# The batch of several experts third, with only its other experts' tokens sorted

## The chip, the cores and the metric

One core of a Trainium2 chip runs the whole kernel. The metric is the time of one execution on the device in microseconds, taken over several runs. The profile is of one further execution; its span goes from the first to the last instruction.

## The reference

Four batches of 10048 tokens of width 128. First attention through 49 agents, then a mixture of 16 experts in four groups of four; each token goes to one group and in it to one expert.

```
a2k = softmax(scale * agents @ k.T);  agent_v = a2k @ v
x = softmax(scale * q @ agents.T) @ agent_v
g = argmax(x @ w_group);  e = argmax(x @ w_expert[g])
out = softmax_g * softmax_e * (relu(x @ w1[g, e]) @ w2[g, e])
```

The drawn inputs (seed 0) send all tokens of three batches to one expert each. The batch numbered 0 in the inputs has 7553 tokens for one expert, 2494 for a second and 1 for a third.

## The kernel before, in words

`PB` gives the order in which the input's batches are computed; below, "batch 0" to "batch 3" (`b`) are places in that order. A batch has 79 columns of 128 tokens, which make 20 FFN tiles of up to 512 tokens (`TILES`, L38).

**Attention.** `agents_of` (L401, lane kind "a") loads keys and values in ten chunks, splits them into two f16 parts on ScalarE (xh) and GpSimd (xl, L290), makes scores, and from them the agents' values. `rest` (L1101, lane kind "q") does the same for the queries (`queries_of`, L629; et is the transposed softmax of a tile), then routing logits, `routing` (L718), the choice of the batch's main expert (`main_of`, L827), the output weights (`output_weight`, L752), `peaks` (L945) and `signed_weights` (L971), which makes the FFN weights: 384 hidden units are computed exactly, the other 640 are taken as of one sign and folded into a linear part.

**FFN.** A tile has three units of `first` (L1119: ph on TensorE, relu to hh on ScalarE, the low part hl on VectorE) and `second` (L1135: po on TensorE), and five `check`s (L1156: pv on TensorE, then neg on ScalarE or a reduction into `flags` on VectorE) that the folded units kept their sign. `natural` (L1187) is a tile of tokens in their own order with the batch's main weights (wbuf); `rows_out` (L1196) scales it, on ScalarE and GpSimd (L1203) where `apart` is true and else on VectorE, and SP stores it (L1208).

**Batch 3 before.** The batch of several experts is last. `taken` (L1481) sorts all its tokens by expert: `leftover` (L1217) gives each token a place by scans, `inverse` (L1340) turns places into row numbers with one-hot products for 82 columns of 128, and up to three experts' weights are made by `prepare_kept` (L1415) and stored in DRAM (wkept). `fetch` (L1420) gathers a tile's rows with four indirect DMAs (er, L1426), `turn` (L1452) transposes them, `scatter` (L1462) stores with four more (L1467). Each is followed by a small memset of gap (`apart`, L1446), and the queue's order is kept. There are 20 whole tiles and one small one; up to five are gathered ahead, and each loads its weights anew from DRAM (`weigh`, L1448).

**What sets the order.** The FFN tiles of batch b are written out one after another, and work of the other lanes is laid between their steps by `run` (L1600) and `advance` (L1573). A lane has a span in units of batches (`SPAN_A`, `SPAN_Q`, `SPAN_O`, `SPAN_F`, L103), a total (`WORK`, L109), and a count of what it has issued: `Counted` (L144) prices each instruction (VectorE 65 + 1.04 per element of a partition, ScalarE 100 + 0.83, TensorE 4 + 0.42), and `WA` weighs TensorE, VectorE and ScalarE. At each step a lane is taken on until its count reaches its share of the total; when its span is over, all that is left of it is issued at once:

```
part = min(1.0, (now - y["start"]) / (y["end"] - y["start"]))
advance(y, part if part < 1 else 1e9, False)
```

Lane "f" is what is left of batch 0's queries and routing, lane "o" is `taken`. The front (to about 86 us) computes batch 0's attention by a written list (`ORDER`). Batches 0 and 1 have 20 natural tiles each, batch 2 has 13 in the same way; then the remaining lanes are finished, and the 21 taken tiles follow with the last seven natural ones of batch 2 among them. While the first two of these tiles run, `prepare_kept` makes the second and third experts' weights. At the end `general` (L1501) looks whether any flag is set or any count was over its limit (`KEPT`, `WHOLE`), and redoes the batches concerned if so.

Of the kernel before, what the change touches and what calls it, by code (L numbers as in the profile page):

```python
# [22 lines left out]
P = 128  # L23
B = 4
# [35 lines left out]
PB = [1, 2, 3, 0]  # L60
LB = B - 1
WHOLE = 20
TAKEN = WHOLE + 1
SOON = TAKEN * TQ
AWAY = 100
KEPT = 3
# [15 lines left out]
BESIDE = 7  # L82
# [20 lines left out]
SPAN_A = {1: (0.3, 0.7), 2: (0.97, 1.4), 3: (1.66, 1.98)}  # L103
SPAN_Q = {1: (0.53, 0.96), 2: (1.34, 1.78), 3: (1.93, 2.34)}
SPAN_O = (2.34, 2.62)
SPAN_F = (0.0, 0.52)
MIX = 2
WA = (0.3, 1.0, 0.3)
WORK = {"a": 25e3, "q": 42e3, "o": 35.7e3, "f": 38e3}  # L109
# [66 lines left out]
def build(ctx, tc, qT, kT, v, agT, wr, w1, w2, cpk, out):  # L176
    nc = tc.nc
    pool, sync = nc.gpsimd, nc.sync
    work = np.zeros(3)
# [43 lines left out]
    flags = const.tile([P, B, TAKEN, SLOTS], F32, name="flags")  # L223
# [30 lines left out]
    pool.memset(wbuf[1], 0)  # L254
# [71 lines left out]
    def key_scores(b, ci):  # L326

        st = state[b]
        S, mch = st["S"], st["mch"]
        t0, t1 = chunks[ci]  # L330
        xh, xl = st.pop(("k", ci))
        ps = bank(b)
        full = t1 - t0 - (1 if t1 == NT else 0)
        for t in range(t0, t1):
            scores(b, ps, xh, xl, t - t0, min(P, N - t * P))
            if t % 4 == 3:
                yield
        act.activation(S[:, t0:t0 + full], ps[:, 0:full * NA].rearrange("p (t a) -> p t a", a=NA), AF.Copy)
        psv = ps[:, 0:(t1 - t0) * NA].rearrange("p (t a) -> p t a", a=NA)
        vec.tensor_reduce(out=mch[:, ci % 2], in_=psv[:, 0:full].rearrange("p t a -> p a t"), axis=AX.X, op=ALU.max)  # L340
        if t1 == NT:
            act.activation(S[0:LAST, NT - 1], psv[0:LAST, full], AF.Copy)
            vec.tensor_max(out=mch[0:LAST, ci % 2], in0=mch[0:LAST, ci % 2], in1=psv[0:LAST, full])
# [324 lines left out]
    def query_split(b, ci, x, early):  # L668
        t0, t1 = chunks[ci]
        ef = x["ef"][:, 0:t1 - t0]  # L670
        if early and ci % 2 == 0:
            pool.tensor_copy(out=rows[:, t0:t1, 0:NA], in_=ef)
        else:
            act.activation(rows[:, t0:t1, 0:NA], ef, AF.Copy)
        whole = early or b == 0 and ci <= FIRST
        for i in range(0, t1 - t0, t1 - t0 if whole else 3):
            y = slice(i, t1 - t0 if whole else min(i + 3, t1 - t0))
            w = slice(t0 + y.start, t0 + y.stop)
            (vec if whole else pool).tensor_sub(out=rows[:, w, NA:2 * NA], in0=ef[:, y], in1=rows[:, w, 0:NA])  # L679
        yield  # L680

    def query_turn(b, ci, x, early):
        t0, t1 = chunks[ci]
        for h0 in range(t0, t1, TQ):
# [4 lines left out]
            et = (mo.tile([2 * NA, TS], F16, name="ett", bufs=4) if b == LB else etp.tile([2 * NA, TS], F16, name="et"))[:, 0:(h1 - h0) * P]  # L689
# [205 lines left out]
    def left_of(b, ps):  # L895
# [4 lines left out]
        lf = sm.tile([1, 2], F32, name="lf")  # L900
        vec.tensor_reduce(out=lf[:, 0:1], in_=lm, axis=AX.X, op=ALU.add)
        vec.tensor_scalar(out=lf[:, 0:1], in0=lf[:, 0:1], scalar1=-1.0, scalar2=float(N), op0=ALU.mult, op1=ALU.add)
        if b:
            vec.tensor_max(out=lf[:, 1:2], in0=lf[:, 0:1], in1=state[b - 1]["info"][:, 1:2])
        else:
            vec.tensor_copy(out=lf[:, 1:2], in_=lf[:, 0:1])
        info = const.tile([1, 2], I32, name=f"info{b}")
# [193 lines left out]
    def rest(b):  # L1101

        if b == LB:
            yield from queries_of(b, None, None, logits_of)
        else:
# [90 lines left out]
    def rows_out(x):  # L1196
# [14 lines left out]
        for y in ins:  # L1211
            if b < LB:
                tc.declare_no_dep(y.ins, group="taken", reason="those rows are of the last batch")
# [206 lines left out]
    def fetch(b, j, name="slot"):  # L1420
# [41 lines left out]
    def scatter(x):  # L1462
# [3 lines left out]
        for q in range(n):  # L1466
# [6 lines left out]
            if group == "taken":  # L1473
                tc.declare_no_dep(ins.ins, group="natural", reason="the rows are of the last batch, or none")
# [26 lines left out]
    def general():  # L1501
# [36 lines left out]
        pe.matmul(ps[:, 0:B * TAKEN], ones16, wrong, start=True, stop=True)
        state["right"] = const.tile([P, B, TAKEN], F16, name="right")
        psb = ps[:, 0:B * TAKEN].rearrange("p (b w) -> p b w", w=TAKEN)  # L1540
        vec.tensor_scalar(out=state["right"], in0=psb, scalar1=0.0, scalar2=None, op0=ALU.is_equal)
# [44 lines left out]
    def lane(kind, b, gen, span):  # L1586
        lanes.append(dict(kind=kind, b=b, gen=gen, start=span[0], end=span[1], total=WORK[kind] - (6.5e3 if kind == "q" and b == LB else 0), done=0.0, until=0.0))
# [10 lines left out]
    lane("o", LB, taken(LB), SPAN_O)  # L1598
    lanes.sort(key=lambda y: y["start"])
    def run(x, at=None, then=None, also=None):  # L1600

        steps = plan(x)
        for k, (kind, i) in enumerate(steps):
# [15 lines left out]
            for y in lanes:  # L1619
                if now > y["start"]:  # L1620
# [7 lines left out]
        if also:  # L1628
            all_of(also)
# [54 lines left out]
```

## Time and profile before

| what | us |
|---|---|
| median of three runs | 991.37 |
| lowest and highest of them | 990.78, 993.18 |
| the profiled execution | 987.76 |
| its span | 985.9 |
| TensorE busy in the span | 745.1 |
| VectorE busy | 700.1 |
| ScalarE busy | 481.3 |
| GpSimd busy | 499.0 |

PE is TensorE, PEld its weight loads, DVE VectorE, ACT ScalarE, POOL GpSimd, SP the engine that issues most DMAs. A window of the profile gives the busy time of each engine in it and the mean clock granted to TensorE as a share of its full speed. Nearly all compute instructions are recorded under one line (L160, the helper that counts them), so groups are told apart by the names of their tiles.

### The profile page before, as it was taken

The numbers are of one execution on the slowest core, as the hardware profiler recorded it, in microseconds if no ns is written. First come the engines' busy times: TensorE is split into PE (matmuls) and PEld (weight loads), VectorE is DVE, ScalarE is ACT, GpSimd is POOL, SyncE is SP. The second block draws the span as 40 slices with busy tenths as digits, with TensorE's granted clock in tenths as the row PEclk, the third lists the DMA queues.
The fourth block names the chain that finished last, engine by engine and source line by source line (L and its number), as shares of the span: only waits on it lengthen the run. The fifth ranks groups of instructions, "written<-read, shape, count | busy, mean of one in ns | idle before, by whom it ended". The sixth has DMA issues, their size and how long they took to land.

```text
span 985.9 us, 22607 instructions
## 1 busy us (share of the span) xinstructions
PE 745.1 (76%) x8802; PEld 556.5 (56%) x8802; DVE 700.1 (71%) x1738; ACT 481.3 (49%) x892; POOL 499.0 (51%) x805
## 2 busy tenths in 40 slices
PE   7839988999638998957669797479385887676873
PEld 5738656676436766744457575247374664454552
DVE  7787979767985867497755559997966774544553
ACT  5445766785413858936314894234122543333431
POOL 3342357470221919638501672113580588888885
PEclk9959999998858999987779899679787998878887
DMA  9562336731640754146505311332111442332321
GB/s 346 202 239 82 98 125 200 219 99 37 235 154 22 200 182 126 34 153 232 175 26 160 86 47 47 141 103 68 30 37 44 147 124 83 93 101 74 109 73 50
DMA packets 61893, 118.32 MB, mean 120 GB/s; under 512 B 7062, under 2 KB 38888, under 8 KB 61392
## 3 DMA queue, kind: packets, MB, share of 16 engines
q1 hardware_dynamic: 56592, 109.55, 34.2%
q0 software_dynamic: 5184, 7.23, 2.9%
q8 instruction: 71, 1.16, 0.5%
q14 instruction: 46, 0.38, 0.1%
HBM read 84.90 MB, written 32.01 MB: 119 GB/s over the span
## 4 chain that ended last, share of the span: by engine, by line
POOL 21%; PE 19%; DVE 14%; issue 4%; DMA 3%; ACT 3%; POOLq 0%; SPq 0%; DVEq 0%; ACTq 0%
PE at L160 10%; POOL out L1467 6%; POOL er L1426 5%; POOL xl L290 5%; PE po L160 4%; PE ph L160 3%; POOL gap L1446 3%; PE pv L160 2%; DVE hl L160 2%; DVE spare L160 1%; POOL rows L679 1%; POOL oo L1203 1%; DMA er<-erow,gidx 1%; DMA xf<-qT 1%; DVE pm L160 1%
## 5 line engine op out<-in xcount | busy, mean ns | idle before, releaser
L290 POOL TENSOR_TENSOR xl<-xf,xh 128x256 f16<-128x256 f32 x280 | 187.5, 702 | 168.6 <-ACT xh L160 167.7
L160 DVE SCALAR_TENSOR_TENSOR hl<-ph,hh 128x512 f16<-128x512 f32 (+1 forms) x241 | 163.4, 679 | 127.0 <-ACT hh L160 125.6
L160 ACT ACTIVATE hh<-ph 128x512 f16<-128x512 f32 (+1 forms) x241 | 142.8, 594 | 118.3 <-PE ph L160 117.5
L160 PEld LDWEIGHTS <-hh 128*128 128x128 f16 x1908 | 162.1, 103 | 38.2 <-issue 6.6
L160 PE MATMUL po<-wbuf,hh 128*128 128x128 f16 x1572 | 170.3, 228 | 0.4 <-ACT hh L160 0.3
L160 PE MATMUL po<-wbuf,hl 128*128 128x128 f16 x786 | 152.9, 228 | 18.3 <-DVE hl L160 18.3
L160 DVE CUSTOM_DVE_ANT_0 spare<-neg,pv 128x512 bf16<-128x512 bf16 (+1 forms) x160 | 107.8, 674 | 33.2 <-PE pv L160 27.7
L1203 POOL TENSOR_TENSOR oo<-oo,cw 128x256 f32<-128x256 f32 (+1 forms) x62 | 43.5, 722 | 166.2 <-ACT oo L160 166.2
L160 PE MATMUL ph<-et,wbuf 98*128 98x512 f16 (+1 forms) x360 | 117.6, 407 | 5.8 <-DVE hl L160 3.3
L160 PE MATMUL pv<-et,wbuf 98*128 98x512 f16 (+1 forms) x300 | 112.2, 407 | 10.3 <-DVE flags L160 3.7
L160 ACT ACTIVATE neg<-pv 128x512 bf16<-128x512 f32 (+1 forms) x160 | 95.0, 594 | 50.4 <-PE pv L160 49.2
L160 PEld LDWEIGHTS <-hl 128*128 128x128 f16 x954 | 98.3, 103 | 34.3 <-DVE hl L160 25.5
L1467 POOL DMA_INDIRECT out<-oo,sidx x81 | 80.7, 997 | 48.6 <-DVE oo L160 35.2
L160 PEld LDWEIGHTS <-wbuf 98*128 98x128 f16 x737 | 67.1, 104 | 54.7 <-issue 32.4
L160 ACT ACTIVATE xh<-xf 128x1024 f16<-128x1024 f32 x78 | 81.7, 1049 | 26.8 <-PE at L160 8.9
L1426 POOL DMA_INDIRECT er<-erow,gidx x81 | 83.3, 1029 | 20.4 <-issue 14.3
L160 PEld LDWEIGHTS <-xh 128*128 128x128 f16 x1264 | 62.7, 99 | 19.1 <-issue 8.7
L160 PE MATMUL at<-agh,xl 128*128 128x49 f16 x545 | 58.5, 189 | 13.1 <-POOL xl L290 12.5
L160 PEld LDWEIGHTS <-xl 128*128 128x128 f16 x632 | 53.1, 98 | 22.7 <-POOL xl L290 20.1
L160 PE MATMUL at<-agh,xh 128*128 128x49 f16 x545 | 59.0, 189 | 6.2 <-ACT xh L160 3.1
L160 DVE TENSOR_REDUCE flags<-pv 128x1 f32<-128x512 f32 (+1 forms) x82 | 55.1, 674 | 7.8 <-PE pv L160 7.6
L160 PEld LDWEIGHTS <-et 98*128 98x128 f16 x948 | 47.7, 99 | 20.3 <-issue 10.5
(384 smaller groups left out, 1567.2 us busy)
## 6 DMA issues: line engine op xcount, KB each, us to landing
xf<-qT SPq DMA_DIRECT2D x38, 512.0 KB, 5.2
vf<-v SPq DMA_DIRECT2D x36, 516.0 KB, 4.1
xf<-kT SPq DMA_DIRECT2D x35, 512.0 KB, 4.4
out<-oo SPq DMA_DIRECT2D x57, 256.0 KB, 2.3
erow<-rows SPq DMA_DIRECT2D x3, 1975.0 KB
wsl<-wkept SPq DMA_DIRECT2D x7, 608.0 KB, 3.6
wsg<-wkept SPq DMA_DIRECT2D x7, 608.0 KB
wbuf<-wkept SPq DMA_DIRECT2D x7, 608.0 KB, 3.6
```

The costliest lines, as they stand in the source:

```text
L160: y = f(*a, **k)
L290: eng.tensor_sub(out=xl[:, y], in0=xf[:, y], in1=xh[:, y])
L679: (vec if whole else pool).tensor_sub(out=rows[:, w, NA:2 * NA], in0=ef[:, y], in1=rows[:, w, 0:NA])
L1203: pool.tensor_mul(out=o[:, y], in0=o[:, y], in1=state[b]["cw"][:, t + y.start:t + y.stop].broadcast_to([P, y.stop - y.start, C]))
L1426: ins = pool.indirect_dma_start(out=er[:, q], out_offset=None, in_=erow[b][:, :], in_offset=bass.IndirectOffsetOnAxis(ap=place(b, col + q) ...
L1446: tc.keep_in_program_order(pool.memset(gap, 0.0))
L1467: ins = pool.indirect_dma_start(out=out, out_offset=bass.IndirectOffsetOnAxis(ap=place(x["b"], x["col"] + q)[1], axis=0), in_=o[:, q], in_ ...
```

## The change

The batch of several experts comes third (`MB`). Like the others it runs 20 natural tiles with the weights of its main expert, for all its tokens. `taken(MB)` then sorts the tokens of its other experts alone: five whole tiles and a small one, two kept weights. Their results are scattered over the rows that the natural tiles wrote. This lane "o" lies beside batch 3's tiles 0 to 11, and one taken tile follows each of batch 3's natural tiles 13 to 18. All four batches now take the same path through `rest`. The lanes' spans, totals and weights are new, and GpSimd's instructions for splitting are counted too (`half`). A lane's predecessor is finished as soon as the lane starts.

```diff
-PB = [1, 2, 3, 0]
+PB = [1, 2, 0, 3]
 LB = B - 1
-WHOLE = 20
+MB = B - 2
+WHOLE = 5
 TAKEN = WHOLE + 1
-SOON = TAKEN * TQ
+SOON = 84
-KEPT = 3
+KEPT = 2
-BESIDE = 7
+FROM = 13
...
-SPAN_A = {1: (0.3, 0.7), 2: (0.97, 1.4), 3: (1.66, 1.98)}
-SPAN_Q = {1: (0.53, 0.96), 2: (1.34, 1.78), 3: (1.93, 2.34)}
-SPAN_O = (2.34, 2.62)
-SPAN_F = (0.0, 0.52)
+SPAN_A = {1: (0.1, 0.42), 2: (0.96, 1.25), 3: (1.96, 2.25)}
+SPAN_Q = {1: (0.42, 0.96), 2: (1.25, 1.96), 3: (2.25, 2.96)}
+SPAN_O = (3.0, 3.55)
+SPAN_F = (0.0, 0.25)
-WA = (0.3, 1.0, 0.3)
-WORK = {"a": 25e3, "q": 42e3, "o": 35.7e3, "f": 38e3}
+WA = (0.3, 1.0, 0.5, 0.5)
+WORK = {"a": 41.3e3, "q": 98.6e3, "o": 80.5e3, "f": 37e3}
...
+    half = Counted(nc.gpsimd, work, 3, 80.0, 2.3)
-    flags = const.tile([P, B, TAKEN, SLOTS], F32, name="flags")
+    flags = const.tile([P, B, NW + TAKEN, SLOTS], F32, name="flags")
-        low(pool, PIECE, xf, xh, xl, n)
+        low(half, PIECE, xf, xh, xl, n)
...
-            st["mch"] = sm.tile([P, 2, NA], F32, name="mch")
+            st["mch"] = rt.tile([P, len(chunks), NA], F32, name="mch", tag="hot")
...
-        if ci:
-            vec.tensor_max(out=mch[:, ci % 2], in0=mch[:, ci % 2], in1=mch[:, 1 - ci % 2])
...
-        mx = st["mch"][:, (len(chunks) - 1) % 2]
+        mx = sm.tile([P, NA], F32, name="mx")
+        vec.tensor_reduce(out=mx, in_=st["mch"].rearrange("p c a -> p a c"), axis=AX.X, op=ALU.max)
...
-            et = (mo.tile([2 * NA, TS], F16, name="ett", bufs=4) if b == LB else etp.tile([2 * NA, TS], F16, name="et"))[:, 0:(h1 - h0) * P]
+            et = etp.tile([2 * NA, TS], F16, name="et")[:, 0:(h1 - h0) * P]
...
     def rest(b):
-        if b == LB:
-            yield from queries_of(b, None, None, logits_of)
-        else:
-            yield from queries_of(b)
-            for ci in range(len(chunks)):
-                yield from logits_of(b, ci)
+        yield from queries_of(b, None, None, logits_of)
         yield from routing(b, 0, NTP)
-        if b < LB:
-            yield from main_of(b, NTP)
-            load_weights(b)
+        yield from main_of(b, NTP)
+        load_weights(b)
         yield from output_weight(b)
         yield from peaks(b)
-        if b < LB:
-            yield from signed_weights(b, wbuf[b % 2], state[b].pop("wf"))
+        yield from signed_weights(b, wbuf[b % 2], state[b].pop("wf"))
...
-        return dict(b=b, w=w, t=t, n=n, per=1, units=FULL, et=state[b]["et", w], apart=b > 0 and (b < LB - 1 or w < NW - BESIDE - 2),
+        return dict(b=b, w=w, t=t, n=n, per=1, units=FULL, et=state[b]["et", w], apart=b > 0 and (b < LB or w < NW - 2),
...
-    def leftover(b, gs, oh=None):
+    def leftover(b, gs, small=False):
         st = state[b]
-        small = oh is not None
-        if oh is None:
-            oh = rt.tile([P, NE, NTP], F16, name="loh", tag="oh")
-            sync.dma_start(out=oh, in_=ohd[b])
-        if b < LB:
+        oh = rt.tile([P, NE, NTP], F16, name="loh", tag="oh")
+        sync.dma_start(out=oh, in_=ohd[b])
+        yield
+        if small:
+            other = sm.tile([P, NE], F16, name="other")
+            vec.tensor_scalar(out=other, in0=st["main"], scalar1=-1.0, scalar2=1.0, op0=ALU.mult, op1=ALU.add)
+            vec.tensor_mul(out=oh, in0=oh, in1=other.unsqueeze(2).broadcast_to([P, NE, NTP]))
+            yield
+        else:
...
     def taken(b):
-        yield from leftover(b, TQ * P, state[b]["oh"][:, NG:])
+        yield from leftover(b, TQ * P, True)
...
+        yield from inverse(b, 0, WHOLE * TQ + 2, columns)
         yield from prepare_kept(b, 0, ws)
-        yield from inverse(b, 0, WHOLE * TQ + 2, columns)
+        yield from prepare_kept(b, 1, wbuf[b % 2])
...
-                    if prior and prior[0]["gen"] and (part > 0.6 or y["b"] == LB):
+                    if prior and prior[0]["gen"]:
                         advance(prior[0], 1e9)
...
+    def take():
+        x = taking.pop(0)
+        if late:
+            weigh(late[0])
+            taking.append(late.pop(0))
+        run(x, None, taking[0] if taking else None)
-    for b in range(LB):
+    for b in range(B):
         for y in lanes:
-            if y["b"] == b and y["gen"] and y["kind"] not in "of":
+            if y["b"] == b and y["gen"] and y["kind"] in "aq":
                 advance(y, 1e9)
-        for w in range(NW - BESIDE if b == LB - 1 else NW):
+        for w in range(NW):
...
-            run(natural(b, w), b + w / NW)
-    for y in lanes:
-        advance(y, 1e9)
-    ring.extend([rt.tile([P, WCI], I32, name="wsl", tag="lg"), rt.tile([P, WCI], I32, name="wsg", tag="S"), wbuf[1]])
-    late.extend(fetch(LB, j, "kept") for j in range(DEPTH))
-    weigh(late[0])
-    beside = [natural(LB - 1, w) for w in [*range(NW - BESIDE, NW - 2), NW - 1, NW - 2]]
-    run(beside.pop(0), None, late[0], prepare_kept(LB, 1, wbuf[1]))
-    for j in range(TAKEN):
-        x = late.pop(0)
-        if late:
-            weigh(late[0])
-        run(x, None, late[0] if late else None, prepare_kept(LB, j + 2, wbuf[1]) if j + 2 < KEPT else None)
-        if (j + 1) * (BESIDE - 2) // TAKEN > j * (BESIDE - 2) // TAKEN:
-            run(beside.pop(0))
-    run(beside.pop(0))
+            soon = b == LB and w == FROM - 1
+            if soon:
+                advance(next(y for y in lanes if y["kind"] == "o"), 1e9)
+                ring.extend([rt.tile([P, WCI], I32, name="wsl", tag="lg"), rt.tile([P, WCI], I32, name="wsg", tag="S"), wbuf[MB % 2]])
+                late.extend(fetch(MB, j, "kept") for j in range(DEPTH))
+                weigh(late[0])
+                taking.append(late.pop(0))
+            run(natural(b, w), b + w / NW, taking[0] if soon else None)
+            if b == LB and FROM <= w < FROM + TAKEN:
+                take()
```

## Rows read from the trace of the kernel before

**Rows 1.** The page: its head and the engines' busy time

```profile
span 985.9 us, 22607 instructions
PE 745.1 (76%) x8802; PEld 556.5 (56%) x8802; DVE 700.1 (71%) x1738; ACT 481.3 (49%) x892; POOL 499.0 (51%) x805
```

**Rows 2.** Windows by stage: length, busy us per engine (instructions), clock, DMA share, GB/s

```profile
0.00:86.00 86.00, 59.00 (x883) 50.84 (x883) 64.13 (x209) 39.66 (x66) 27.59 (x46) 0.82 0.63 232
86.00:314.00 228.00, 183.21 (x2384) 138.48 (x2384) 184.66 (x459) 130.28 (x247) 89.82 (x154) 0.88 0.43 135
314.00:623.00 309.00, 244.79 (x3290) 181.41 (x3288) 219.32 (x495) 189.69 (x359) 156.09 (x262) 0.91 0.38 118
623.00:712.00 89.00, 62.56 (x530) 45.10 (x530) 80.09 (x217) 27.25 (x49) 24.55 (x23) 0.81 0.26 91
712.00:773.00 61.00, 45.36 (x303) 37.31 (x304) 41.19 (x129) 16.42 (x33) 22.98 (x37) 0.79 0.14 44
773.00:976.00 203.00, 150.19 (x1420) 103.39 (x1416) 110.69 (x234) 77.97 (x139) 177.75 (x285) 0.87 0.34 100
976.00:986.00 10.00, 0.00 (x0) 0.00 (x0) 0.00 (x0) 0.00 (x0) 0.25 (x2) 0.50 0.03 6
```

**Rows 3.** Windows of other stretches, same columns

```profile
100.00:250.00 150.00, 133.37 (x1951) 98.63 (x1947) 122.75 (x306) 105.16 (x200) 70.88 (x128) 0.94 0.43 130
250.00:310.00 60.00, 32.88 (x260) 26.04 (x258) 47.16 (x115) 14.73 (x25) 12.84 (x16) 0.69 0.46 155
325.00:425.00 100.00, 90.77 (x1360) 68.26 (x1361) 67.96 (x148) 77.75 (x150) 62.31 (x113) 1.00 0.44 129
600.00:773.00 173.00, 119.61 (x960) 90.31 (x959) 144.16 (x392) 50.90 (x95) 52.29 (x66) 0.81 0.21 69
86.00:976.00 890.00, 686.10 (x7921) 505.69 (x7920) 635.97 (x1530) 441.60 (x827) 471.19 (x759) 0.87 0.36 110
```

**Rows 4.** Timeline of SP's queue, 285 to 330 us: start, us, line, issue

```profile
292.55 0.56 SPq L1210 DMA_DIRECT2D out<-oo  x1
...
326.99 0.40 SPq L1208 DMA_DIRECT2D out<-oo  x1
```

**Rows 5.** Groups of instructions of GpSimd, 796 to 956 us

```profile
L1467 POOL DMA_INDIRECT out<-oo,sidx x59 | 59.0, 1000 | 9.9 <-issue 9.5 <-DVE hl L160 0.2 <-DVE flags L160 0.2
L1426 POOL DMA_INDIRECT er<-erow,gidx x53 | 54.2, 1022 | 10.5 <-issue 9.9 <-PE ph L160 0.5 <-PE pv L160 0.2
L1446 POOL MEMSET gap<- 128x160 f16 x111 | 28.1, 253 | 0.1
```

**Rows 6.** Groups of VectorE, 773 to 976 us: the scaling of finished tiles

```profile
L160 DVE TENSOR_TENSOR oo<-po,er 128x512 f32<-128x512 f32 (+1 forms) x20 | 13.3, 665 | 0.2 <-PE po L160 0.2
...
L160 DVE TENSOR_TENSOR oo<-po,cw 128x512 f32<-128x512 f32 (+1 forms) x6 | 4.0, 659 | 1.1 <-DMA out<-oo,sidx 1.1
```

**Rows 7.** Window of two tiles of the last stage, columns as in rows 2

```profile
830.20:841.60 11.40, 10.36 (x114) 7.43 (x114) 8.23 (x17) 6.24 (x11) 10.07 (x17) 1.00 0.45 143
```

**Rows 8.** Windows of tile hot alone: length, PE, PEld and DVE busy

```profile
712.00:773.00 61.00, 23.61 (x112) 4.67 (x48) 9.73 (x32) 0.79 0.14 44
```

**Rows 9.** Windows of tile hl alone, same columns

```profile
314.00:623.00 309.00, 60.89 (x321) 32.27 (x321) 54.89 (x81) 0.91 0.38 118
623.00:712.00 89.00, 15.39 (x76) 8.28 (x76) 12.81 (x19) 0.81 0.26 91
712.00:773.00 61.00, 5.76 (x27) 2.95 (x27) 5.49 (x8) 0.79 0.14 44
```

**Rows 10.** Waits of TensorE, 623 to 773 us: total us, times, longest

```profile
PE at L160 <- DVE cntf L160: 23.2, 3, 10.9
```

**Rows 11.** Tiles er and oo: min/median/max ns, first and last start

```profile
L1426 POOL DMA_INDIRECT er<-erow,gidx x81: 1002/1005/1342, 708.5 to 951.2; - x81
...
L1467 POOL DMA_INDIRECT out<-oo,sidx x81: 977/983/1027, 772.9 to 975.0; - x81
L1203 POOL TENSOR_TENSOR oo<-oo,cw x62: 399/612/2538, 325.8 to 668.8; 128x256 f32<-128x256 f32 x61, 128x128 f32<-128x128 f32 x1
```

More of the change, by code (lines that the diff above doesn't have):

```diff
@@ L178, in build @@
     pool, sync = nc.gpsimd, nc.sync
-    work = np.zeros(3)
+    work = np.zeros(4)
     pe = Counted(nc.tensor, work, 0, 4.0, 0.42)
@@ L253, in build @@
     wbuf = [const.tile([P, WCI], I32, name=f"wbuf{i}") for i in range(2)]
-    pool.memset(wbuf[1], 0)
+    pool.memset(wbuf[MB % 2], 0)
     erow = [dram.tile([P * NT, RW], I32, name=f"erow{i}") for i in range(B)]
@@ L339, in key_scores @@
         psv = ps[:, 0:(t1 - t0) * NA].rearrange("p (t a) -> p t a", a=NA)
-        vec.tensor_reduce(out=mch[:, ci % 2], in_=psv[:, 0:full].rearrange("p t a -> p a t"), axis=AX.X, op=ALU.max)
+        vec.tensor_reduce(out=mch[:, ci], in_=psv[:, 0:full].rearrange("p t a -> p a t"), axis=AX.X, op=ALU.max)
         if t1 == NT:
             act.activation(S[0:LAST, NT - 1], psv[0:LAST, full], AF.Copy)
-            vec.tensor_max(out=mch[0:LAST, ci % 2], in0=mch[0:LAST, ci % 2], in1=psv[0:LAST, full])
-        if ci:
-            vec.tensor_max(out=mch[:, ci % 2], in0=mch[:, ci % 2], in1=mch[:, 1 - ci % 2])
+            vec.tensor_max(out=mch[0:LAST, ci], in0=mch[0:LAST, ci], in1=psv[0:LAST, full])
         yield
@@ L678, in query_split @@
             w = slice(t0 + y.start, t0 + y.stop)
-            (vec if whole else pool).tensor_sub(out=rows[:, w, NA:2 * NA], in0=ef[:, y], in1=rows[:, w, 0:NA])
+            (vec if whole else half).tensor_sub(out=rows[:, w, NA:2 * NA], in0=ef[:, y], in1=rows[:, w, 0:NA])
         yield
@@ L899, in left_of @@
         vec.tensor_mul(out=lm, in0=ps[0:1], in1=st["main"][0:1])
-        lf = sm.tile([1, 2], F32, name="lf")
+        lf = sm.tile([1, 1], F32, name="lf")
         vec.tensor_reduce(out=lf[:, 0:1], in_=lm, axis=AX.X, op=ALU.add)
         vec.tensor_scalar(out=lf[:, 0:1], in0=lf[:, 0:1], scalar1=-1.0, scalar2=float(N), op0=ALU.mult, op1=ALU.add)
-        if b:
-            vec.tensor_max(out=lf[:, 1:2], in0=lf[:, 0:1], in1=state[b - 1]["info"][:, 1:2])
-        else:
-            vec.tensor_copy(out=lf[:, 1:2], in_=lf[:, 0:1])
-        info = const.tile([1, 2], I32, name=f"info{b}")
+        info = const.tile([1, 1], I32, name=f"info{b}")
         vec.tensor_copy(out=info, in_=lf)
@@ L1211, in rows_out @@
         for y in ins:
-            if b < LB:
-                tc.declare_no_dep(y.ins, group="taken", reason="those rows are of the last batch")
+            if b != MB:
+                tc.declare_no_dep(y.ins, group="taken", reason="those rows are of another batch")
                 tc.add_to_no_dep_group("natural", y.ins)
-    def leftover(b, gs, oh=None):
+    def leftover(b, gs, small=False):
         st = state[b]
-        small = oh is not None
-        if oh is None:
-            oh = rt.tile([P, NE, NTP], F16, name="loh", tag="oh")
-            sync.dma_start(out=oh, in_=ohd[b])
-        if b < LB:
+        oh = rt.tile([P, NE, NTP], F16, name="loh", tag="oh")
[7 more added lines that the diff above has]
+        else:
             held = rt.tile([P, NTP], F16, name="held")
@@ L1437, in fetch @@
             per = min(TQ // w, FULL)
-            x.update(per=per, units=-(-FULL // per), **signed(j, TQ // w, MODES if w == TQ else "DD"))
+            x.update(per=per, units=-(-FULL // per), **signed(NW + j, TQ // w, MODES if w == TQ else "DD"))
         else:
@@ L1473, in scatter @@
             if group == "taken":
-                tc.declare_no_dep(ins.ins, group="natural", reason="the rows are of the last batch, or none")
+                tc.declare_no_dep(ins.ins, group="natural", reason="the rows are of another batch, or none")
             tc.add_to_no_dep_group(group, ins.ins)
@@ L1532, in general @@
         every = None
-        bad = rt.tile([P, B, TAKEN], F32, name="bad")
+        bad = rt.tile([P, B, NW + TAKEN], F32, name="bad")
         vec.tensor_reduce(out=bad, in_=flags, axis=AX.X, op=ALU.max)
-        wrong = rt.tile([P, B * TAKEN], F16, name="wrong")
+        wrong = rt.tile([P, B * (NW + TAKEN)], F16, name="wrong")
         vec.tensor_scalar(out=wrong, in0=bad.rearrange("p b w -> p (b w)"), scalar1=0.0, scalar2=None, op0=ALU.is_gt)
         ps = bank(1)
[L1538 to L1541, printed above, removed]
+        pe.matmul(ps[:, 0:B * (NW + TAKEN)], ones16, wrong, start=True, stop=True)
+        psb = ps[:, 0:B * (NW + TAKEN)].rearrange("p (b w) -> p b w", w=NW + TAKEN)
+        state["right"] = const.tile([P, B, NW], F16, name="right")
+        vec.tensor_scalar(out=state["right"], in0=psb[:, :, 0:NW], scalar1=0.0, scalar2=None, op0=ALU.is_equal)
         most = const.tile([1, B + 1], F32, name="most")
@@ L1586, in lane @@
     def lane(kind, b, gen, span):
-        lanes.append(dict(kind=kind, b=b, gen=gen, start=span[0], end=span[1], total=WORK[kind] - (6.5e3 if kind == "q" and b == LB else 0), done=0.0, until=0.0))
+        lanes.append(dict(kind=kind, b=b, gen=gen, start=span[0], end=span[1], total=WORK[kind], done=0.0, until=0.0))
     all_of(main_row(0))
@@ L1597, in build, with run @@
         lane("q", b, rest(b), SPAN_Q[b])
-    lane("o", LB, taken(LB), SPAN_O)
+    lane("o", LB, taken(MB), SPAN_O)
     lanes.sort(key=lambda y: y["start"])
-    def run(x, at=None, then=None, also=None):
+    def run(x, at=None, then=None):
         steps = plan(x)
@@ L1611, in run @@
                     second(*pending.pop(0))
-            if also:
-                for _ in range(3):
-                    next(also, None)
             if at is None:
@@ L1624, in run @@
                     part = min(1.0, (now - y["start"]) / (y["end"] - y["start"]))
-                    if prior and prior[0]["gen"] and (part > 0.6 or y["b"] == LB):
+                    if prior and prior[0]["gen"]:
                         advance(prior[0], 1e9)
                     advance(y, part if part < 1 else 1e9, False)
-        if also:
-            all_of(also)
-    for b in range(LB):
+    taking = []
+    def take():
[5 more added lines that the diff above has]
+    for b in range(B):
         for y in lanes:
-            if y["b"] == b and y["gen"] and y["kind"] not in "of":
+            if y["b"] == b and y["gen"] and y["kind"] in "aq":
                 advance(y, 1e9)
-        for w in range(NW - BESIDE if b == LB - 1 else NW):
+        for w in range(NW):
             y = next(y for y in lanes if y["kind"] == "f")
```

1 line of the change is left out of this document (removed).

## The prediction

> **What bounds the kernel now.** I read the page first: the span is 985.9 us, and no engine is full in it; TensorE is busy for 76%, VectorE for 71%, GpSimd for 51% [rows 1]. So I cut the span into stages at the times at which the outputs of a batch leave, and asked for the busy time of each engine in each [rows 2]. Of the 890 us between the front and the end TensorE is busy for 686, a share of 0.77 [rows 3]. Where FFN tiles run beside attention work, the share is 0.89 (100 to 250 us) and 0.91 (325 to 425 us); where a batch is being prepared it is 32.9 of 60 us, 0.55, and 119.6 of 173 us, 0.69 [rows 3].
>
> Two causes show. **First, the lanes.** A "q" lane is planned with a total of 42,000 units. Counting its instructions with the kernel's own prices gives about 55,000 of VectorE, 37,000 of ScalarE times 0.3 and 21,000 of TensorE times 0.3, some 73,000. So its planned part ends soon after the queries, and when the lane's end comes, the other 30,000 (output weights, peaks, signed weights) run in one piece. In the trace the last output of the first batch leaves at 292.6 us and the first one of the next at 327.0 us [rows 4]: 34 us in which the next weights are not there. **Second, the last stage.** From 773 to 976 us GpSimd is busy for 177.8 of 203 us [rows 2]. A taken tile issues four gathers and four scatters, each with a memset behind it: 8 x (about 1.01 + 0.25 + 0.17 idle) = 11.4 us on the one queue [rows 5]. TensorE and VectorE wait for it.
>
> **The change part by part, in TensorE time.** TensorE is nearest to full where work mixes, so I sum its busy time per stage and divide by a share.
>
> *A tile.* The last stage has 26 tiles (20 scaled by er, 6 by cw [rows 6]) and 150.2 us of TensorE [rows 2]: 5.8 us each. At a granted clock of 1.00, the higher of its two levels (2.4 GHz), two tiles took 10.36 us [rows 7], 5.2 each; that is the lower end. On VectorE it is 110.7 / 26 = 4.3 us. The count of tiles goes from 60 + 20 and a small one to 80 + 5 and a small one: the drawn inputs send 7553 tokens of the moved batch to one expert, 2494 to a second, 1 to a third, so five whole tiles remain to be sorted.
>
> *A set of signed weights.* From 712 to 773 us two sets are made (32 hot instructions, 16 a set [rows 8]) beside 8 hl, that is 2.7 tiles [rows 9]. TensorE: 45.4 - 2.7 x 5.8 = 30, so 15 us a set. VectorE: 41.2 - 2.7 x 4.3 = 30, also 15. The number of sets stays at six: one more main set, one less kept.
>
> *Leftover and inverse.* From 623 to 712 us: 62.6 us of TensorE, less 19 hl (6.3 tiles, 37 us) and one set (15), leaves 11. VectorE: 80.1 - 27 - 15 = 38; the inverse now compares 22 columns rather than 82, which can only lower that.
>
> *First batch* (86 to 314 us): 183.2 us of TensorE, the same work after. *Second and third:* from 314 to 623 us before there are 27 tiles (81 hl [rows 9]), two batches' attention and one set, 244.8 us. After there are 40 tiles and two sets: 244.8 + 13 x 5.8 + 15 = 335. *Last:* 26.25 tiles x 5.8 = 152, two kept sets 30, leftover and inverse 11: 193 us. VectorE has there at most 113 + 30 + 38 = 181, so TensorE still leads. Together 712, where there were 686: five more tiles cost 29 us and the dropped gathers' transposes are inside the 5.8.
>
> *Share.* After, a lane's total of 98,600 agrees with the same count at the new factors (55,000 + 6,400 + half of 37,000 + half of 39,000 of GpSimd = 99,500), so a lane's work is laid evenly over its span and little is left for its end. Between 0.80 (the first batch now, 183.2 / 228) and 0.91 I take 0.88, close to the mixed stretches, a little under for the hand-overs. In the last batch I add two waits of TensorE for cntf, 23.2 / 3 = 7.7 us each [rows 10], though the lane now pauses there.
>
> **The sum:** front 86, first batch 183.2 / 0.88 = 208, second and third 335 / 0.88 = 381, last 193 / 0.88 + 15 = 235, end 10 [rows 2]: a span of 920. The profiled execution took 987.8 us for its span of 985.9, and the median of the runs is 3.6 above that, so I add 5.5: **925 us**.
>
> *Edits at nothing.* Key maxima kept per chunk and reduced once: about as much VectorE as before. Their buffer now shares a slot with hot, so a batch's first key maximum waits for the last hot product of the batch before; the lanes are in that order already, and if not, the wait is the end of one set. The one-hot table of the sorted batch is read back on SP's queue, ahead of output DMAs, and its waiting delays only outputs, which have four buffers. Scaling by GpSimd goes on until tile 17 of the last batch: two instructions a tile. The five prefetched tiles put 20 gathers (28 us at 1.42) ahead of them on GpSimd's queue, while four output buffers at 6.6 us a tile cover 26; if that cover is gone, ScalarE stalls by what is over, a few us.
>
> *What gathers do beside VectorE.* Here a gather takes 1002 to 1342 ns and a scatter 977 to 1027 [rows 11], with VectorE busy for 55% of that stage [rows 2]; 42 of them at 1.42 are 60 us beside 14 tiles (94 us), hidden.
> The Trainium skill (SBUF — State Buffer, "A bandwidth-pool intuition that's wrong (but worth ruling out)") says that a DMA issued by GpSimd takes about 620 ns alone and 3100 ns beside a VectorE copy that holds the shared port. By that rule as an estimate the 42 would need 42 x (3.1 + 0.42) = 148 us, and the sum would be 54 us higher; the trace before shows no such indirect DMA.
>
> **The rivals.**
> *A, the forecast*, 925 us, own range 890 to 950. For it: one stretch of 150 us and one of 100 already run at this share with VectorE at 82% and 68% [rows 3].
> *B, the last batch does not mix.* Leftover, inverse and two sets are a chain of small dependent steps, and the old stage with such steps ran at 0.69 [rows 3], the taken one at 150.2 / 203 = 0.74. Then 12 tiles, the sets and the leftover take (70 + 41) / 0.69 = 160 us and the other 14.25 tiles 83 / 0.74 = 112: 272 in place of 235, so 962 us. Against it: the lane has 11 tiles to lie beside, not 5.
> *C, slower: the share of 0.77 does not rise.* The change then only adds five tiles: 712 / 0.77 + 96 = 1020 in the span, some 1025 us. Its place is TensorE's queue, which runs in the written order: every lane step that waits holds the FFN matmuls behind it, whatever the lanes' totals are. It decides below a share of 712 / 890 = 0.80. For it: the first three batches together had no more than that. Against it: their loss lies at the lanes' ends, not throughout.
> *D, the change does not do what it says.* Kept weights are now chosen with the peaks of the batch computed after theirs; if a sign check fails, the general path redoes tiles, at least one more stage of 203 us [rows 2], over 1100 us. The checks guard each sign, and the hardest 384 units are exact, so I give it little.
> *E, faster still: the clock.* It stood at 0.88 and 0.91 in the first batches and at 0.79 from 712 to 773 us [rows 2]; if the pauses go, a tile costs 5.2, and at a share of 0.91 the stages give 201 + 360 + 210, a span of 867, 873 us.
> *F, GpSimd still binds the end.* Its longest scaling took 2.54 us where the median is 0.61 [rows 11]; if each indirect DMA grew to that beside a busier VectorE, 42 x (2.54 + 0.42) = 124 us against the 94 of the tiles: 955 us.
> The Trainium skill (SBUF — State Buffer, the section named above) states such a lock; this is what it would be in this kernel.
>
> **How the numbers follow.** A 0.58, B 0.16, F 0.04, E 0.07, C 0.12 (0.03 of it within the bound, where the share is just under 0.80), D 0.03. A measurement of this kernel tells about 0.3% from no change, 3 us. Faster: A, B, F and E, 0.85; the same 0.03; slower 0.12. The range from 875 to 985 holds A, B, F and most of E; outside are most of C, D and a little of E, under 0.2.
>
> **What would show it.** Right: 256 hl rather than 241; 21 gathers and 21 scatters; no stretch with GpSimd over 85%; TensorE's share from the front to the end at 0.85 or more, without stretches like the one at 250 us; about 208, 190, 190 and 235 us for the four batches; at most two waits for cntf of some us in the last. Wrong: a share near 0.77 in the first three batches (C), 270 us for the last (B), indirect DMAs of 2 us and more (F), or instructions behind the last check (D).

## The result and the profile after

The changed kernel takes 914.5 us, median of four runs (912.0 to 915.9), against 991.9 for the kernel before: a ratio of 0.9216, 95% interval 0.9193 to 0.9240. The span of its profiled execution is 912.9 us where 920 were summed. The total was met by terms that missed in both directions, so how close it came is luck.

The page of the changed kernel, its head and the engines' busy time, as in [rows 1]:

```profile
span 912.9 us, 22711 instructions
PE 745.9 (82%) x9007; PEld 562.4 (62%) x9007; DVE 693.1 (76%) x1742; ACT 494.4 (54%) x929; POOL 369.0 (40%) x619
```

TensorE has as much to do as before, in 73 us less. GpSimd's time alone fell by much, 130 us.

Windows of the changed kernel, columns as in [rows 2]. The borders are the last outputs of the first three batches, a point just before the end of the sorting lane (its last set is stored at 829 us), and the last output:

```profile
86.00:326.00 240.00, 196.15 (x2458) 145.26 (x2456) 186.38 (x456) 134.23 (x257) 92.53 (x160) 0.87 0.40 127
326.00:522.00 196.00, 162.70 (x2066) 120.84 (x2063) 144.07 (x336) 117.86 (x227) 88.92 (x151) 0.91 0.40 124
522.00:716.00 194.00, 167.08 (x1968) 123.62 (x1966) 143.69 (x336) 111.70 (x217) 76.39 (x133) 0.89 0.32 98
716.00:822.00 106.00, 83.58 (x742) 63.12 (x740) 88.25 (x259) 38.81 (x72) 44.60 (x68) 0.84 0.19 54
822.00:902.00 80.00, 78.13 (x892) 58.95 (x891) 65.64 (x147) 50.83 (x93) 37.72 (x63) 1.00 0.35 105
902.00:913.00 11.00, 0.00 (x0) 0.00 (x0) 0.30 (x2) 0.00 (x0) 0.00 (x0) 0.66 0.09 24
86.00:902.00 816.00, 687.63 (x8113) 511.79 (x8110) 628.03 (x1531) 453.43 (x862) 340.16 (x573) 0.89 0.35 108
```

| term | forecast, us | measured, us |
|---|---|---|
| front | 86 | 86 |
| first batch | 208 | 240 |
| second and third | 381 | 196 + 194 = 390 |
| last batch | 235 | 106 + 80 = 186 |
| end | 10 | 11 |

The count of tiles tells where the time went. A whole tile has three hl. First the windows of tile hl alone in the kernel before, to the start of its last stage and in it:

```profile
86.00:773.00 687.00, 128.72 (x661) 67.91 (x661) 113.63 (x168) 0.88 0.36 114
773.00:976.00 203.00, 57.32 (x295) 30.34 (x293) 49.77 (x73) 0.87 0.34 100
```

and then in the changed kernel, split at 822 us:

```profile
86.00:822.00 736.00, 164.70 (x824) 86.10 (x824) 142.63 (x211) 0.88 0.35 108
822.00:902.00 80.00, 33.62 (x187) 18.19 (x187) 30.48 (x45) 1.00 0.35 105
```

Before, 73 hl or 24.3 tiles passed in the last 203 us: 8.3 us each. After, 45 hl or 15 tiles passed in 80 us: 5.3 each, TensorE busy for 78.1 of them at full clock. That excess, 3.0 x 24.3 = 73 us, is as large as the whole gain. The rest cancels: five more tiles cost 5 x 5.3 = 27 us, the end is 1 us longer, and the long part before the last stage takes 14.3 more tiles for only 49 us more, which is 27 less than 14.3 x 5.3.

TensorE's idle time divides the gain differently. In the last stage it falls from 53 of 203 us to 2 of 80, in the part before that stage from 151 of 687 us to 126 of 736 (busy times of [rows 2] and of the windows above): 51 us less in the one, 25 in the other. The last stage is thus most of the gain by either count, but a part of some 25 us lies before it.

Groups of GpSimd in the changed kernel, 822 to 902 us (columns as in [rows 5]):

```profile
L1461 POOL DMA_INDIRECT out<-oo,sidx x21 | 20.7, 984 | 17.1 <-DVE oo L161 14.4 <-issue 2.6
L1193 POOL TENSOR_TENSOR oo<-oo,cw 128x256 f32<-128x256 f32 x18 | 10.7, 622 | 30.8 <-ACT oo L161 30.8
L1440 POOL MEMSET gap<- 128x160 f16 x22 | 5.6, 252 | 0.0
```

GpSimd now waits for VectorE and ScalarE to finish a tile (14.4 and 30.8 us); in [rows 5] its idle time was "issue", the step from one instruction to the next.

### The profile page after: what moved, and what is told of

Same layout as the page of the kernel before. It is cut to its first block, busy times and chain, and to the rows that moved or that the text cites. A ratio compares the mean times of both kernels' runs of the same rounds, so it can differ in the third digit from the quotient of the medians.

```text
span 912.9 us, 22711 instructions
## 1 busy us (share of the span) xinstructions
PE 745.9 (82%) x9007; PEld 562.4 (62%) x9007; DVE 693.1 (76%) x1742; ACT 494.4 (54%) x929; POOL 369.0 (40%) x619
## 5 line engine op out<-in xcount | busy, mean ns | idle before, releaser
L161 POOL TENSOR_TENSOR xl<-xf,xh 128x256 f16<-128x256 f32 (+2 forms) x276 | 183.0, 697 | 159.8 <-ACT xh L161 108.3
L161 PE MATMUL po<-wbuf,hl 128*128 128x128 f16 x963 | 189.7, 230 | 35.8 <-DVE hl L161 35.8
L161 PE MATMUL po<-wbuf,hh 128*128 128x128 f16 x1926 | 211.3, 229 | 1.6 <-ACT hh L161 1.4
L1193 POOL TENSOR_TENSOR oo<-oo,cw 128x256 f32<-128x256 f32 x116 | 75.5, 672 | 234.4 <-ACT oo L161 227.5
L161 PE MATMUL ph<-et,wbuf 98*128 98x512 f16 x480 | 160.9, 419 | 5.9 <-DVE hl L161 2.9
L161 PE MATMUL pv<-et,wbuf 98*128 98x512 f16 (+1 forms) x400 | 149.9, 420 | 7.0 <-DVE hl L161 5.2
L161 PEld LDWEIGHTS <-et 98*128 98x128 f16 x1264 | 67.4, 101 | 29.1 <-issue 13.7
L161 PE MATMUL po<-wbuf,et 98*128 98x128 f16 x632 | 56.2, 230 | 10.5 <-ACT oo L161 9.5
L161 ACT ACTIVATE oo<-po 128x512 f32<-128x512 f32 (+1 forms) x58 | 34.9, 601 | 44.3 <-PE po L161 31.6
L161 POOL TENSOR_TENSOR rows<-ef,rows 128x147 f16<-128x147 f32 (+1 forms) x108 | 42.8, 426 | 36.6 <-ACT rows L161 26.4
```

Source lines behind the costliest of these rows:

```text
L161: y = f(*a, **k)
L1193: pool.tensor_mul(out=o[:, y], in0=o[:, y], in1=state[b]["cw"][:, t + y.start:t + y.stop].broadcast_to([P, y.stop - y.start, C]))
```

## The experiments

The runs were made on several chips. Each ratio is to the kernel before on the run's own chip, and only runs of one chip are compared to a few us.

**Is it GpSimd's queue? The memset twice, before and after.** In `apart`, in both kernels:

```diff
         tc.keep_in_program_order(pool.memset(gap, 0.0))
+        tc.keep_in_program_order(pool.memset(gap, 0.0))
```

> The kernel before with the small memset behind each indirect DMA written twice (0.25 us each). Queue theory (from 773 to 976 us every taken tile waits for 11.4 us of GpSimd's queue): some 18 tiles of eight indirect DMAs pay it in full, 18 x 8 x 0.25 = 36 us, so 1020 to 1032 us. Rival (TensorE, or the landing of the gathers, bounds that stage and GpSimd is only busy beside it): under 10 us, 985 to 1002 us.

> The changed kernel with the same memset twice. Queue theory: 42 x 0.25 = 10.5 us more on a GpSimd that is now busy for under half of the last 80 us, so hidden: within 4 us of the changed kernel, 911 to 919 us. Rival F of the prediction (GpSimd still binds the end): 8 to 11 us slower, 922 to 926 us.

Before: 1040.7 us, 51 more than the 989.7 of the kernel before on that chip, ratio 1.052 (1.046 to 1.057). After: 913.5 us, ratio 0.9216 (0.9169 to 0.9262), the same as without. The first lies above the 1020 to 1032 us expected. Groups of GpSimd in before_gap_twice, 820 to 1010 us:

```profile
L1468 POOL DMA_INDIRECT out<-oo,sidx x58 | 57.9, 998 | 16.2 <-issue 15.0 <-DVE oo L160 0.6 <-DVE hl L160 0.6
L1426 POOL DMA_INDIRECT er<-erow,gidx x47 | 48.0, 1021 | 9.5 <-issue 9.5
L1447 POOL MEMSET gap<- 128x160 f16 x111 | 26.8, 241 | 3.5
L1446 POOL MEMSET gap<- 128x160 f16 x111 | 26.7, 241 | 3.4
```

GpSimd still idles for little but "issue". With its step to the next instruction a memset costs 0.24 + 0.03; 162 of them are 44 us. The kernel paid that and a little more. This fits a queue that was in the way for nearly all its length, and not for 18 tiles alone as the expectation had it. In the changed kernel 42 such memsets cost nothing that can be measured: rival F falls.

**The scatters off the queue.** In `scatter` of the kernel before:

```diff
+        if x["group"] == "taken":
+            at = PB[x["b"]] * N + min(x["j"] * TQ * P, N - n * P)
+            sync.dma_start(out=out[at:at + n * P].rearrange("(q p) c -> p q c", p=P), in_=o[:, 0:n])
-        for q in range(n):
+        for q in range(0 if x["group"] == "taken" else n):
```

> The kernel before with the taken tiles stored by one plain DMA each on SP's queue rather than four scatters on GpSimd's, so their rows are left in sorted order: the placing of the rows is left out. GpSimd then needs 4 x 1.42 = 5.7 us a tile. Queue theory: the stage falls from 8.35 us a tile (203 us, 24.3 tiles) to 5.3 to 6, the changed kernel's last stage took 80 us for 15 tiles: 50 to 70 us less, 920 to 945 us. Lane theory (the pauses in the first 770 us are the loss): 970 us or more.

This kernel leaves out the placing of the rows, and with the scatters their memsets go too. 926.5 us, ratio 0.934 (0.929 to 0.939): 63 us gone, with the lanes and the tiles of before. Its last stage, all engines and then tile hl alone:

```profile
773.00:916.00 143.00, 132.30 (x1488) 97.83 (x1487) 115.93 (x252) 81.54 (x147) 76.24 (x123) 0.97 0.49 148
773.00:916.00 143.00, 54.63 (x304) 29.59 (x304) 51.74 (x76) 0.97 0.49 148
```

76 hl in 143 us are 5.6 us a tile. TensorE's share rises from the 0.74 of [rows 2] to 0.93 and its clock from 0.87 to 0.97, though not one of its instructions was changed; what was changed is the stores and GpSimd's queue. This is the clearest single test of the study.

**Is it the lanes? Full totals in the kernel before.**

```diff
-SPAN_A = {1: (0.3, 0.7), 2: (0.97, 1.4), 3: (1.66, 1.98)}
-SPAN_Q = {1: (0.53, 0.96), 2: (1.34, 1.78), 3: (1.93, 2.34)}
+SPAN_A = {1: (0.3, 0.7), 2: (1.0, 1.4), 3: (1.85, 2.08)}
+SPAN_Q = {1: (0.53, 0.96), 2: (1.42, 1.84), 3: (2.05, 2.34)}
-WA = (0.3, 1.0, 0.3)
-WORK = {"a": 25e3, "q": 42e3, "o": 35.7e3, "f": 38e3}
+WA = (0.3, 1.0, 0.5, 0.5)
+WORK = {"a": 41.3e3, "q": 98.6e3, "o": 66e3, "f": 37e3}
...
```

The rest of the edit is cut here: GpSimd's splitting is counted by `half`, the last lane q has 30,000 less than the others (before 6,500), and a lane's predecessor is finished at 0.45 of the lane rather than 0.6.

> The kernel before, with the lanes counted as after (GpSimd's splitting counted, full totals) and the spans of the third and fourth batch moved so that they follow one another; the last stage as it was. Lane theory: the first three batches gain 15 to 30 us, so 962 to 977 us. Queue theory: 985 to 997 us, since the stage from 773 us is as it was.

997.8 us, ratio 1.0066 (1.0033 to 1.0099): no gain, even a little slower. The spans had to be moved as well, so this is not the totals alone; but counting the whole work, with these spans, did not gain 15 us.

**The lanes in the changed kernel: a short total, and its control.**

```diff
-SPAN_A = {1: (0.1, 0.42), 2: (0.96, 1.25), 3: (1.96, 2.25)}
-SPAN_Q = {1: (0.42, 0.96), 2: (1.25, 1.96), 3: (2.25, 2.96)}
+SPAN_A = {1: (0.1, 0.42), 2: (1.0, 1.29), 3: (2.0, 2.29)}
+SPAN_Q = {1: (0.42, 0.96), 2: (1.29, 1.96), 3: (2.29, 2.96)}
...
-WORK = {"a": 41.3e3, "q": 98.6e3, "o": 80.5e3, "f": 37e3}
+WORK = {"a": 41.3e3, "q": 57e3, "o": 80.5e3, "f": 37e3}
```

The last two lines are q_total_short's alone.

> The changed kernel with the total of lane q at 57,000 in place of 98,600 (the same part of the full count as 42,000 was before), and with lanes a of the third and fourth batch starting at the batch's border (1.0 and 2.0). To be compared with a_later, which has the second edit alone. Lane theory (laying a lane's whole work evenly over its span is a main part of the gain): the preparing comes in one piece again at 0.96, 1.96 and 2.96, and the kernel is 15 to 40 us slower than a_later. Queue theory (the gain is the last stage's GpSimd queue, the lanes' totals count little): within 5 us of a_later.

> The changed kernel with lanes a of the third and fourth batch starting at 1.0 and 2.0 rather than 0.96 and 1.96, and their lanes q at 1.29 and 2.29. Both theories: within 6 us of the changed kernel, 909 to 921 us, since these lanes start only 0.8 of a tile later. It is the control for q_total_short.

q_total_short takes 907.2 us, 0.9147 (0.9125 to 0.9169); a_later 900.8, 0.9069 (0.9035 to 0.9103). On the same chip the short total costs 6.4 us: between the two expectations, just over the 5 us of the queue's and far under the 15 of the lanes'. The piece in which the preparing comes is plain in the window from 266 to 306 us, first of q_total_short, then of a_later:

```profile
266.00:306.00 40.00, 9.89 (x55) 8.70 (x56) 34.93 (x93) 4.77 (x7) 7.55 (x8) 0.54 0.56 193
```

```profile
266.00:306.00 40.00, 27.70 (x177) 20.55 (x175) 33.25 (x88) 8.81 (x16) 4.20 (x4) 0.68 0.38 130
```

TensorE is busy for 9.9 us of 40 in the one and 27.7 in the other, and yet the time hardly differs. VectorE is busy for 34.9 and 33.3: it is the full engine there, and the tiles that don't run beside it had run earlier. The windows of tile hl on VectorE up to then, of q_total_short and then of a_later, have 58 hl and 48:

```profile
86.00:266.00 180.00, 39.25 (x58) 0.94 0.39 119
```

```profile
86.00:266.00 180.00, 32.79 (x48) 0.93 0.41 129
```

A stretch with an idle TensorE is no loss by itself.

The control missed: 14 us under the changed kernel where 6 were allowed. So the start of the next batch's keys matters more than was thought; its granted clock is 0.904 where the changed kernel had 0.888, and no one wait of the trace carries the 14 us. The last outputs of the four batches are issued at these times (us):

| kernel | first | second | third | last |
|---|---|---|---|---|
| the changed one | 325.8 | 522.1 | 714.9 | 901.7 |
| a_later | 323.0 | 517.5 | 703.8 | 890.4 |
| a_later_still, below | 322.0 | 522.2 | 720.3 | 910.1 |
| a_later_from14, below | 320.3 | 510.3 | 695.9 | 883.8 |

Some 6 us of a_later's gain lie in the third batch. It beats both kernels. Moved on by another 1.2 tiles:

```diff
-SPAN_A = {1: (0.1, 0.42), 2: (1.0, 1.29), 3: (2.0, 2.29)}
-SPAN_Q = {1: (0.42, 0.96), 2: (1.29, 1.96), 3: (2.29, 2.96)}
+SPAN_A = {1: (0.1, 0.42), 2: (1.06, 1.35), 3: (2.06, 2.35)}
+SPAN_Q = {1: (0.42, 0.96), 2: (1.35, 1.96), 3: (2.35, 2.96)}
```

> a_later with lanes a of the third and fourth batch moved by another 1.2 tiles, to 1.06 and 2.06, and their lanes q to 1.35 and 2.35. If a_later gained because the next batch's keys no longer mix with the preparing of the weights before them, all of that was had at 1.0, and this is within 4 us of a_later (897 to 905 us). If it is a matter of where the lanes' work falls beside the tiles, the time moves on by 5 us or more, either way.

923.7 us, 0.8937 (0.8888 to 0.8985), on a chip on which the kernel before took 1034.1. That is 24 more than a_later_from14 (below) there. The table above puts all of it before the last batch (720.3 against 695.9 us), where those two kernels differ only by this shift. So it is where the work falls beside the tiles, and a good start lies in a narrow stretch. Why, stays open.

**The first batch, 32 us over the forecast.** The changed kernel with the first batch's spans of before:

```diff
-SPAN_A = {1: (0.1, 0.42), 2: (0.96, 1.25), 3: (1.96, 2.25)}
-SPAN_Q = {1: (0.42, 0.96), 2: (1.25, 1.96), 3: (2.25, 2.96)}
-SPAN_F = (0.0, 0.25)
+SPAN_A = {1: (0.3, 0.7), 2: (0.96, 1.25), 3: (1.96, 2.25)}
+SPAN_Q = {1: (0.53, 0.96), 2: (1.25, 1.96), 3: (2.25, 2.96)}
+SPAN_F = (0.0, 0.52)
```

> The changed kernel with the first batch's spans of before (f to 0.52, a from 0.3 to 0.7, q from 0.53). The first batch took 240 us where 208 were forecast. If f and a crowded into its first tiles are the cause: 10 to 20 us faster, 895 to 905 us. If the loss lies in the preparing at its end (250 to 318 us, where VectorE is busy for 45 of 50 us), the shorter span of q makes that no better: 911 to 922 us.

919.7 us, 0.9270 (0.9245 to 0.9295): the second outcome. Crowding in its first tiles is not the cause. Its first batch ends at 331 us, that of the changed kernel at 326. Spans between the two, on a_later:

```diff
-SPAN_A = {1: (0.1, 0.42), 2: (1.0, 1.29), 3: (2.0, 2.29)}
-SPAN_Q = {1: (0.42, 0.96), 2: (1.29, 1.96), 3: (2.29, 2.96)}
-SPAN_F = (0.0, 0.25)
+SPAN_A = {1: (0.2, 0.5), 2: (1.0, 1.29), 3: (2.0, 2.29)}
+SPAN_Q = {1: (0.5, 0.98), 2: (1.29, 1.96), 3: (2.29, 2.96)}
+SPAN_F = (0.0, 0.35)
```

> a_later with the first batch's lanes between the two plans tried (f to 0.35, a 0.2 to 0.5, q 0.5 to 0.98). If the first batch's 240 us are set by the sum of its work, TensorE 193 and VectorE 186 us, and not by its order: within 4 us of a_later, 897 to 905 us. If by the order: 890 us or less, or 908 us or more.

894.3 us, ratio 0.8636 (0.8590 to 0.8682), on that same chip. It is the lowest time of a kernel that leaves nothing out, between the two expectations, and 6 us under a_later_from14 on that chip, where their intervals overlap; so it doesn't tell the two causes apart. Part of the 32 us is only the border. The kernel before, counted to its first output of the second batch at 327 us, was as long:

```profile
86.00:327.00 241.00, 195.08 (x2577) 146.85 (x2577) 195.91 (x484) 142.60 (x269) 98.67 (x169) 0.89 0.42 132
```

The forecast's 183 us of TensorE went to 314 us only. By 327 us it was 195, for 66 hl on VectorE; the changed kernel has 196 and 63 hl by 326. So the change made the first batch no faster, and the gain of 20 us forecast for it did not come.

**What the sorting costs.** The changed kernel without the lane "o" and its tiles:

```diff
+        state[MB]["info"] = none
...
-    lane("o", LB, taken(MB), SPAN_O)
+    none = const.tile([1, 2], I32, name="over")
+    pool.memset(none, 0)
...
-            soon = b == LB and w == FROM - 1
+            soon = False
...
-            if b == LB and FROM <= w < FROM + TAKEN:
-                take()
```

> The changed kernel without the sorting of the other experts' tokens: leftover, inverse, two kept sets and the six taken tiles are left out (2495 tokens keep the main expert's result). By the sum: 5.25 tiles at 5.3 is 28 us, and the first 12 tiles of the last batch, 106 us with the lane, take 12 x 5.5 = 66 without: together 68 us, so 840 to 855 us. If the lane mostly fills time that VectorE had free: 870 us or more.

814.5 us: the sorting costs 100 us, not 68, and the time is under both expectations. (On this chip after_gap_twice, as fast as the changed kernel, took 913.5.) The last batch of that kernel, all engines and then tile hl alone:

```profile
716.00:810.00 94.00, 92.15 (x1062) 67.70 (x1058) 75.33 (x166) 62.21 (x112) 21.32 (x36) 1.00 0.19 57
716.00:810.00 94.00, 42.13 (x235) 22.73 (x234) 38.92 (x57) 1.00 0.19 57
```

19 tiles in 94 us are 4.9 each, TensorE full at full clock and VectorE at 75 of 94 us. Tiles alone thus leave VectorE little room: of the 100 us, 5.25 tiles are 26 to 28, and some 70 go to leftover, inverse and two sets, which the prediction had priced at 41 us of TensorE.

**A longer lane for it.** On a_later:

```diff
-FROM = 13
+FROM = 14
...
-SPAN_O = (3.0, 3.55)
+SPAN_O = (3.0, 3.6)
```

> a_later with the sorting lane spread over one tile more (3.0 to 3.6) and the taken tiles beside tiles 14 to 19. If the last batch is bound by the sum of VectorE's work (some 154 of 187 us), a longer spread gains 0 to 5 us (895 to 901 us). If the lane's chain of small steps makes TensorE wait, fewer steps fall to each tile and it gains more, 5 to 12 us.

900.0 us, 0.8701 (0.8648 to 0.8754), against a_later's 900.8 on another chip, so only roughly: the first outcome, at its small end, if the two chips are alike for it. With the row of 716 to 822 us above, VectorE busy for 88 of 106, the last batch's preparing seems bound by VectorE; no run shows it.

**The memset made small.** In `apart` of the kernel before:

```diff
-        tc.keep_in_program_order(pool.memset(gap, 0.0))
+        tc.keep_in_program_order(pool.memset(gap[:, 0:2], 0.0))
```

> The kernel before with the memset behind each indirect DMA cut to two columns; another memset that small took 0.12 us, against 0.25. Queue theory: 0.13 x 150 = 20 us less, 966 to 976 us. Rival (the stage follows TensorE or the gathers' landing): within 4 us of the kernel before.

1050.0 us against 1034.1 for the kernel before on the same chip, ratio 1.0135 (1.0079 to 1.0192): both theories missed, the queue's even in its direction. The waits of this kernel from 773 to 1000 us (engine and line waiting, releaser, total us, times, longest):

```profile
PEld L160 <- issue: 112.7, 169, 10.5
POOL out L1467 <- DVE oo L160: 95.0, 9, 45.5
PE po L160 <- issue: 38.1, 57, 1.2
```

Here GpSimd waits for the tiles (95 us), and TensorE for nothing that the profile shows ("issue"). The first of these rows in the kernel before, in the same window, is small:

```profile
PEld L160 <- issue: 14.9, 54, 0.3
```

In [rows 5] GpSimd's idle time was its own "issue". On this chip the last stage of this kernel is thus held in part by TensorE's own issuing, for a cause that stays open, and the run is no test of the queue on the others. That the old kernel itself is 43 us slower there, and two variants of the changed one (894 and 900 us) are not, fits a last stage that is bound differently; there is no trace of the unedited kernel on that chip to show it.

## Why the prediction was right, and where its steps were not

**The second cause was the right one.** "TensorE and VectorE wait for it": before_plain_store shows it by taking work off the queue, before_gap_twice by adding some, and after_gap_twice shows that the changed kernel is free of it, all on one chip. before_gap_small, on another, does not fit and is not explained.

The wait itself is in the traces. TensorE waits for gathered rows in the last stage of the kernel before, and longer in before_gap_twice:

```profile
PE at L160 <- DMA er<-erow,gidx: 42.1, 37, 2.8
```

```profile
PE at L160 <- DMA er<-erow,gidx: 63.1, 50, 3.6
```

In before_plain_store and in the changed kernel it does not wait for them.

**The first cause, the lanes, was over-weighted.** The trace has the pieces that were named, and q_total_short brings them back, but they are worth 6 us. That is the price of lane q's total alone: moving the spans a little changed the time by 14 us and by 24, and what the new spans and totals are worth together no run shows. The step that failed is the one on the share: 0.88 was taken "close to the mixed stretches" because little would be left for a lane's end. The measured share from the front to the end is 687.6 / 816 = 0.84, where 0.85 was asked for, and the stretch that was to vanish is still there. The changed kernel from 250 to 300 us, in two windows:

```profile
250.00:275.00 25.00, 14.19 (x91) 9.60 (x90) 24.37 (x56) 7.83 (x13) 7.48 (x8) 0.64 0.64 220
275.00:300.00 25.00, 19.07 (x113) 13.53 (x112) 20.57 (x65) 5.79 (x10) 0.00 (x0) 0.68 0.32 114
```

VectorE is busy for 45 of 50 us, so the preparing of a batch looks bound by it. Then "a share of TensorE" was the wrong unit for these stretches, and VectorE's sum the bound to price; this is argued from the windows, no run shows it.

**Two terms were mis-sized, one each way.** The first batch: 183 us of TensorE at 0.88, measured 196 at 0.82 (to a later border, as said above). The last batch: 193 us of TensorE, measured 83.6 + 78.1 = 162. About half of the 31 us between is the price of a tile: 5.8 us was taken from a stage that was itself slowed to a mean clock of 0.87; the low end, 5.2 from the two tiles at full clock, is what the last 80 us show (78.1 / 15 = 5.2). The price of a tile had been read from the stage that the change removes. Another 11 us is their number: 26.25 were summed, but 20 natural tiles, five whole ones and a small one are 25.3 (76 hl), and three of these hl lie before 716 us. That "TensorE still leads" holds for the batch, 162 us to 154, but not beside the sorting lane, 84 to 88. The two waits for cntf, added at 15 us, came to 5.3 in the last batch:

```profile
PE at L161 <- DVE cntf L161: 5.3, 2, 4.5
```

**The rest.** The counts are as forecast: 211 + 45 = 256 hl, 21 gathers and 21 scatters. No tile follows the last check, so rival D did not come about. Rival C is excluded by the share of 0.84, though the first batch alone came near its 0.80. Rival B had its place right (the sorting lane is the dearest part of the last batch, 106 us) but not its price: 186 us in place of 272. Of E the full clock came true, in the last 80 us alone. As to the rule of the Trainium skill (SBUF — State Buffer, "A bandwidth-pool intuition that's wrong (but worth ruling out)") on GpSimd's DMAs beside VectorE: a gather still took 1.0 to 1.35 us in the changed kernel, as this row of tile er shows, so nothing like its 3.1 us was met. Of the 21 gathers 20 ran before 822 us, beside a VectorE busy for 88 of 106 us; the scatters ran behind it, at a mean of 0.98 us with VectorE at 66 of 80. Which of VectorE's instructions here would hold the port, no run shows.

```profile
L1420 POOL DMA_INDIRECT er<-erow,gidx x21: 1002/1005/1350, 754.0 to 860.0; - x21
```

**Open.** The 27 us that the part before the last stage gives back have no experiment of their own; the inverse of 22 columns, one kept set less, and the new spans and totals together are candidates. Open too are the cause of a_later's 14 us and what slows TensorE in before_gap_small.

## What to carry to other kernels

Divide each stage by the units of work in it and look for the stage with the dear unit: 8.3 us a tile, against 4.9 to 5.3 in the stretches that have little else than tiles, named the loss, while bringing back the pauses that stood out in the busy shares cost 6 us. Price a step from a stretch that is not held by what the change removes. More arithmetic of a cheap, regular kind (five more tiles, 27 us) can be a good price for taking a serial queue of small DMAs off the path.

## What was not expected of the hardware

The same kernel before took 990 to 992 us on three occasions and 1034 on the chip of the last four runs, while a variant of the changed kernel (a_later_from14) took 900 there and its nearest relative (a_later) 901 on another chip. And TensorE's clock changed where only other engines had: in before_plain_store the same matmuls ran at a mean of 0.97 where they had 0.87. In the changed kernel it stood at the lower of its levels (1.2 GHz) from 650 to 670 us, where VectorE is busy for 16.8 of 20 us. Before that TensorE had been busy for 27 of 30 us from 600 to 630, at 1.00, and for 13 of 20 from 630 to 650:

```profile
650.00:670.00 20.00, 15.55 (x84) 10.96 (x84) 16.82 (x29) 3.76 (x7) 1.68 (x2) 0.50 0.29 115
```
